# Strassen's seven products for eight in the second feed-forward's first weights, with the tokens in two passes

## The chip, the cores and the metric

The kernel runs on one core of a Trainium2 chip. The metric is the device time in microseconds (us); three runs of the kernel before give 2407.78, 2408.85 and 2410.29, median 2408.85. The engines are TensorE (PE; PEld is its weight load), VectorE (DVE), ScalarE (ACT), GpSimd (POOL) and SyncE (SP), whose queue issues the DMA transfers.

## The reference

Attention over 4 batches of 8 heads, 576 positions of 64, masked by blocks of 64; then two feed-forwards on 2304 tokens of 512 values. The change touches the last one alone: eight experts, all of them on every token, weighted by a matrix P that eight rounds of row and column normalisation make of the logits.

```
logits = x @ w_gate                         # 2304 x 8
P = exp(logits - logits.max())
for _ in range(8):
    P /= P.sum(1, keepdims=True) + 1e-09
    P /= P.sum(0, keepdims=True) + 1e-09
    P *= N / E
for e in range(8):
    h = np.maximum(x @ w1[e], 0.0)          # 512 -> 1024
    out += P[:, e:e + 1] * (h @ w2[e])      # 1024 -> 512
```

## The kernel before

**Numbers.** Products run in fp32r. Each operand is split into a high part (a copy to fp32r, `copy`, line 274 on ScalarE, 278 on VectorE) and a low part (what is left, `minus`, line 287 on GpSimd or VectorE). A product is three matmuls, high by high, high by low, low by high (`THREE`).

**Order.** Every operation is put into a graph with its engine, an estimated duration and the buffers that it reads and writes. `Graph.emit` then makes the order of each engine by a list schedule, twelve times forward and backward, and keeps the shortest by its own estimates. An operation with alternatives goes to the engine on which it would end first. So the order of every engine is fixed before the run, each works through its own in order, and waits for others by semaphores. Buffers are rings: the next use of a ring's tile waits for the users of the one before.

**The second feed-forward, `moe2`.** The 2304 tokens lie in five blocks (512, 512, 512, 384, 384), with the 512 values as four chunks of 128 partitions, in the tiles `acc`. `split_x2` makes high and low parts of all five blocks, `x2`. The weights come in 32 rounds: 8 experts by 4 groups `g`, each of two slices `f` of 128 hidden values. A round loads four tiles of 128 x 512 (two of w1, two of w2; ring `raw`, 3 tiles) by SP and splits them (`Loader.get`; ring `w`, 9 tiles). Then, for each block:

- `up` (its matmuls on line 881, in `xw`): for each `f`, 4 chunks by 3 terms = 12 matmuls into one PSUM bank `ps`, as wide as the block; then ScalarE's relu writes the high part of `h` (line 1088) and VectorE its low part (line 1090).
- `down` (line 1103), one block behind: for each 128 tokens 6 matmuls of 512 columns into a bank `pm`, which VectorE multiplies by P and adds into `acc` (line 1118). So `acc` first holds x and then the output.

The `logits` (line 1022) are made of the split x as 16 rows and turned back by transposes (line 1032). `sink` makes P during the first rounds.

Of the kernel before, what the change touches and what calls it, by code (L numbers as in the profile page):

```python
# [8 lines left out]
F32 = mybir.dt.float32  # L9
# [181 lines left out]
def t_act(n, psum=False, ap=0):  # L191
    return (50 if psum else 92) + n / 1.2 + 90 * ap


def t_v1(n):
    return 66 + n / 0.96
# [19 lines left out]
def tile_attn_moe_moe2(ctx: ExitStack, tc: tile.TileContext, qT, kT, vP, wg, wv, wo, rg, gw, w1, w2, ident_d, mq_d, mk_d, bm_d, out):  # L216
# [14 lines left out]
    def f32(ap):  # L231
        return ap.bitcast(F32)
# [736 lines left out]
    def late_buf(make, par=False):  # L969
        b = Buf(late(make), par=par)  # L970
        b.before = set(att_ops)
        return b

    def moe2():
        x2 = []
        for j in range(NB):
            n = BL[j]
            if j < NB - 1:
                b = late_buf(lambda p, j=j, n=n: p.tile([128, 2 * NK * n], F32R, name=f"x2_{j}"), par=True)
            else:  # L980
                b = XT.next(par=True)
            x2.append(b)
        gwr = late_buf(lambda p: p.tile([128, NK, E], F32, name="gwr"))
        gws = late_buf(lambda p: p.tile([128, NK, 128], F32R, name="gws"))
        onec = late_buf(lambda p: p.tile([128, 128], F32, name="onec"))
        lg = late_buf(lambda p: p.tile([128, TT, 2 * E], F32, name="lg"), par=True)
        Pm = late_buf(lambda p: p.tile([128, TT, E], F32, name="Pm"))
        sm1 = late_buf(lambda p: p.tile([128, TT], F32, name="sm1"))
        sm8 = late_buf(lambda p: p.tile([128, E], F32, name="sm8"))
        sc1 = late_buf(lambda p: p.tile([128, 8], F32, name="sc1"))  # L990
        lt_t = late(lambda p: p.tile([2 * E, 512], F32, name="lt"))
        LT = Ring([lt_t])

        def x2v(j):
            return x2[j]()[:, 0 : 2 * NK * BL[j]].rearrange("p (c k n) -> p c k n", c=2, k=NK)

        def split_x2(j):
            for k in range(NK):
                hi = Buf(x2[j].get)
                hi.before = x2[j].before  # L1000
                src = accb[j][k]
                h_ = lambda k=k: x2v(j)[:, 0, k]
                copy(G.op, BL[j], h_, src, r=[src], w=[hi])
                x2[j].writes |= hi.writes
                x2[j].users |= hi.writes
                minus(G.op, BL[j], lambda k=k: x2v(j)[:, 1, k], src, lambda h_=h_: f32(h_()), r=[src, hi], w=[x2[j]])

        G.op("SP", 100, lambda: nc.sync.dma_start(out=gwr(), in_=gw), w=[gwr], lat=2000)
        G.op("DVE", 300, lambda: nc.vector.memset(f32(gws()), 0.0), w=[gws])
        G.op("DVE", 100, lambda: nc.vector.memset(onec(), 1.0), w=[onec])  # L1010
        G.op("ACT", t_act(32), lambda: nc.scalar.activation(out=gws()[:, :, 0:E], in_=gwr(), func=AF.Copy), r=[gwr, gws], w=[gws])
        G.op("DVE", t_v1(32), lambda: nc.vector.tensor_tensor(
            out=gws()[:, :, E : 2 * E], in0=gwr(), in1=f32(gws()[:, :, 0:E]), op=ALU.subtract), r=[gwr, gws], w=[gws])

        def logits(j):
            n, nt, t0 = BL[j], BL[j] // 128, B0[j] // 128
            ps, lt = PO.next(), LT.next()

            def go():
                for k in range(NK):  # L1020
                    for c in range(2):
                        nc.tensor.matmul(out=ps()[:, 0:n], lhsT=gws()[:, k, :], rhs=x2v(j)[:, c, k, :],  # L1022
                                         start=k == 0 and c == 0, stop=k == NK - 1 and c == 1)

            G.op("PE", 8 * t_mm(n), go, r=[gws, x2[j]], w=[ps], prio=1.0)
            G.op("ACT", t_act(n, True), lambda: nc.scalar.activation(out=lt()[:, 0:n], in_=ps()[0 : 2 * E, 0:n], func=AF.Copy),
                 r=[ps], w=[lt])
            pt = PO.next()

            def tp():  # L1030
                for t in range(nt):
                    nc.tensor.transpose(out=pt()[:, 2 * E * t : 2 * E * (t + 1)], in_=lt()[:, 128 * t : 128 * t + 128],
                                        identity=ident_t[0 : 2 * E, 0 : 2 * E])

            G.op("PE", 110 * nt, tp, r=[lt, ident], w=[pt], prio=1.0)
            G.op("ACT", 150, lambda: nc.scalar.activation(
                out=lg()[:, t0 : t0 + nt, :], in_=pt()[:, 0 : 2 * E * nt].rearrange("p (t e) -> p t e", t=nt), func=AF.Copy),
                r=[pt], w=[lg])

        def sink():  # L1040

            V = nc.vector

            def first():
                V.tensor_tensor(out=Pm(), in0=lg()[:, :, 0:E], in1=lg()[:, :, E : 2 * E], op=ALU.add)
                V.tensor_reduce(out=sc1()[:, 0:1], in_=Pm().rearrange("p t e -> p (t e)"), axis=AX, op=ALU.max)

            G.op("DVE", 500, first, r=[lg], w=[Pm, sc1])
# [7 lines left out]
            G.op("ACT", 1600, lambda: nc.scalar.activation(out=Pm(), in_=Pm(), func=AF.Exp, bias=sc1()[:, 2:3], scale=1.0),  # L1056
                 r=[Pm, sc1], w=[Pm])
# [21 lines left out]

        accc = [[fixed(acc[j][:, DM * t : DM * t + DM]) for t in range(BL[j] // 128)] for j in range(NB)]  # L1080

        def up(e, g, j, ws):
            n, hs = BL[j], []
            xv = lambda: x2v(j)
            for w in ws:
                ph, ht = PS.next(), HT.next()
                xw(ph, w, [x2[j]] * NK, xv, n, 2.0)
                G.op("ACT", t_act(n, True), lambda ph=ph, ht=ht: nc.scalar.activation(  # L1088
                    out=ht()[:, 0, 0:n], in_=ph()[:, 0:n], func=AF.Relu), r=[ph], w=[ht])
                G.op("DVE", t_v1(n), lambda ph=ph, ht=ht: nc.vector.scalar_tensor_tensor(  # L1090
                    out=ht()[:, 1, 0:n], in0=ph()[:, 0:n], scalar=0.0, in1=f32(ht()[:, 0, 0:n]),
                    op0=ALU.max, op1=ALU.subtract), r=[ph, ht], w=[ht])
                hs.append(ht)
            return hs

        def down(e, g, j, hs, ws):
            for t in range(BL[j] // 128):
                tt, dst, y = B0[j] // 128 + t, accc[j][t], PM.next()

                def go(t=t, y=y):  # L1100
                    for q, ht in enumerate(hs):
                        for a, c in THREE:
                            nc.tensor.matmul(  # L1103
                                out=y(), lhsT=ht()[:, a, 128 * t : 128 * t + 128], rhs=ws[q]()[:, c, :],
                                start=q == 0 and (a, c) == (0, 0), stop=q == len(hs) - 1 and (a, c) == (1, 0))

                G.op("PE", 3 * len(hs) * t_mm(512), go, r=[*hs, *ws], w=[y], prio=2.0)
                if e == 0 and g == 0:
                    G.op("ACT", t_act(512, True), lambda y=y, dst=dst: nc.scalar.activation(out=dst(), in_=y(), func=AF.Copy),
                         r=[y], w=[dst], after=x2[j].writes)  # L1110
                elif e == 0:
                    G.op("DVE", t_v1(512), lambda y=y, dst=dst: nc.vector.tensor_tensor(out=dst(), in0=y(), in1=dst(), op=ALU.add),
                         r=[y, dst], w=[dst])
                else:
                    if e == 1 and g == 0:
                        G.op("DVE", 63 + t_v2(512), lambda dst=dst, tt=tt: nc.vector.tensor_scalar_mul(
                            out=dst(), in0=dst(), scalar1=Pm()[:, tt, 0:1]), r=[dst, Pm], w=[dst])
                    G.op("DVE", 63 + t_v1(512), lambda y=y, dst=dst, tt=tt, e=e: nc.vector.scalar_tensor_tensor(  # L1118
                        out=dst(), in0=y(), scalar=Pm()[:, tt, e : e + 1], in1=dst(), op0=ALU.mult, op1=ALU.add),
                        r=[y, dst, Pm], w=[dst])  # L1120
                if e == E - 1 and g == NG - 1:
                    G.op("SP", 1100, lambda dst=dst, tt=tt: nc.sync.dma_start(out=out[128 * tt : 128 * tt + 128, :], in_=dst()), r=[dst])

        pend = None
        for e in range(E):
            for g in range(NG):
                fs = range(GF * g, GF * g + GF)
                w1s = [L.get(w1[e, f], None, False, 0.5) for f in fs]
                w2s = None
                for j in range(NB):  # L1130
                    if e == 0 and g == 0:
                        split_x2(j)
# [67 lines left out]
```

## Time and profile before

| | |
|---|---|
| median of three runs | 2408.85 us |
| the profiled execution, its own time | 2405.6 us |
| its span, first to last instruction | 2403.8 us |
| mean granted TensorE clock | 0.982 |
| PE busy | 2340.4 us, 97% |
| VectorE, ScalarE, GpSimd busy | 1250.0, 632.2, 488.6 us |

The profile shows one execution. Its time and its span differ by what lies around the instructions. Busy shares are means over stages with different limits: in the first third of the span the attention keeps VectorE, ScalarE and GpSimd busy too, from about 800 us on the second feed-forward runs. Matmuls are pipelined, so the duration of one (some 0.4 us for 512 columns) is longer than the step from one start to the next; the price of a matmul is read from starts.

### The profile page before, as it was taken

To read this page: it belongs to the slowest core of one execution; us is meant where nothing else is said; L and a number is where in the kernel's file an instruction comes from. 1 tells how busy PE (TensorE), PEld (TensorE's weight loads), DVE (VectorE), ACT (ScalarE), POOL (GpSimd) and SP (SyncE) were. 2 spreads that over 40 slices of the span, in tenths; PEclk is the share of its full clock that TensorE was granted. 3 is DMA by queue.
4 is the path that set the end of the run, shared out by engine and by line. 5 is a ranking of instruction groups with operands and counts; after the bars stand their busy time and mean duration, and the time that the engine had idled before them with its cause. 6 is when DMAs were issued, how large, how long until landed. Compare 5 with 4: busy or idle time off the path is not lost.

```text
span 2403.8 us, 28223 instructions
## 1 busy us (share of the span) xinstructions
PE 2340.4 (97%) x10918; PEld 1963.0 (82%) x10918; DVE 1250.0 (52%) x2162; ACT 632.2 (26%) x1359; POOL 488.6 (20%) x405
## 2 busy tenths in 40 slices
PE   8789889999999999999999999999999999999999
PEld 5567667888899888888888888888888888888887
DVE  8899987876533623543333433344433443333444
ACT  3566655454212321111111111111111111111110
POOL 5565653422311211000110001100011001110000
PEclk8889999999999999999999999999999999999999
DMA  5544566453576100000000000000000000000002
GB/s 155 153 152 153 185 193 215 152 167 115 201 234 232 48 27 18 27 18 18 27 23 22 18 18 27 27 18 18 18 27 27 18 18 18 27 27 18 18 1 79
DMA packets 70970, 177.76 MB, mean 74 GB/s; under 512 B 12842, under 2 KB 16170, under 8 KB 70836
## 3 DMA queue, kind: packets, MB, share of 16 engines
q1 hardware_dynamic: 70836, 175.96, 23.3%
q8 instruction: 86, 1.41, 0.2%
q14 instruction: 48, 0.39, 0.1%
HBM read 152.33 MB, written 23.59 MB: 73 GB/s over the span
## 4 chain that ended last, share of the span: by engine, by line
PE 84%; DVE 6%; issue 1%; DMA 0%; ACT 0%; POOL 0%; SPq 0%; DVEq 0%; POOLq 0%
PE ps L881 33%; PE pm L1103 33%; PE pm L881 9%; PE pm L912 5%; PE ps L657 1%; PE ps L457 1%; DVE p L649 1%; PE po L700 1%; DVE mn L465 1%; DVE acc L334 1%; DVE ptl L664 1%; DVE acc L336 0%; DVE acc L921 0%; DVE rs L640 0%; PE po L1022 0%
## 5 line engine op out<-in xcount | busy, mean ns | idle before, releaser
L881 PE MATMUL ps<-x,w 128*128 128x512 f32 (+1 forms) x3840 | 835.1, 372 | 0.0
L1103 PE MATMUL pm<-w,h 128*128 128x512 f32 x3456 | 815.7, 391 | 0.0
L881 PEld LDWEIGHTS ps<-x,w 128*128 128x128 f32 x3840 | 703.6, 188 | 108.3
L1103 PEld LDWEIGHTS pm<-w,h 128*128 128x128 f32 x3456 | 647.6, 188 | 136.1
L1090 DVE SCALAR_TENSOR_TENSOR h<-ps,h 128x512 fp32r<-128x512 f32 (+1 forms) x320 | 204.1, 638 | 675.8 <-ACT h L1088 673.6
L1118 DVE SCALAR_TENSOR_TENSOR acc<-pm,Pm,acc 128x512 f32<-128x512 f32 x504 | 378.5, 751 | 242.8 <-PE pm L1103 239.0
L1088 ACT ACTIVATE h<-ps 128x512 fp32r<-128x512 f32 (+1 forms) x320 | 177.6, 555 | 1231.7 <-PE ps L881 1231.7
L287 POOL TENSOR_TENSOR w<-raw,w 128x512 fp32r<-128x512 f32 x161 | 211.6, 1322 | 1382.2 <-ACT w L274 1341.9
L881 PE MATMUL pm<-x,w 128*128 128x512 f32 (+1 forms) x1440 | 335.3, 378 | 2.9 <-POOL x L287 1.3
L881 PEld LDWEIGHTS pm<-x,w 128*128 128x128 f32 x1440 | 258.5, 191 | 35.6 <-DVE acc L921 1.7
L912 PE MATMUL pm<-h,w 128*128 128x512 f32 (+1 forms) x720 | 164.9, 377 | 3.8 <-DVE t L896 1.5
L912 PEld LDWEIGHTS pm<-h,w 128*128 128x128 f32 x720 | 131.6, 192 | 21.7 <-DVE t L896 2.0
L274 ACT ACTIVATE w<-raw 128x512 fp32r<-128x512 f32 x164 | 102.6, 627 | 89.9 <-PE pm L1103 83.4
L287 POOL TENSOR_TENSOR h<-t,h 128x512 fp32r<-128x512 f32 (+1 forms) x56 | 69.2, 1237 | 186.3 <-ACT h L274 178.5
L465 DVE TENSOR_REDUCE mn<-ps 128x1 f32<-128x512 f32 (+4 forms) x159 | 72.9, 474 | 19.5 <-PE ps L457 18.7
L472 ACT ACTIVATE p<-ps,mn 128x128 f32<-128x128 f32 (+3 forms) x142 | 72.5, 517 | 35.5 <-DVE mn L465 28.4
L657 PE MATMUL ps<-ident,p 128*128 128x128 f32 (+1 forms) x370 | 76.2, 291 | 3.6 <-DVE p L649 3.5
L896 DVE SCALAR_TENSOR_TENSOR t<-t,pm 128x512 f32<-128x512 f32 (+1 forms) x60 | 37.6, 627 | 79.4 <-ACT t L894 79.2
L921 DVE TENSOR_TENSOR acc<-pm,acc 128x512 f32<-128x512 f32 (+1 forms) x100 | 63.1, 632 | 28.4 <-PE pm L912 25.9
L657 PEld LDWEIGHTS ps<-ident,p 128*128 128x128 f32 (+1 forms) x370 | 48.7, 148 | 32.5 <-issue 10.2
L457 PE MATMUL ps<-ka,qa 128*128 128x512 f32 (+3 forms) x150 | 54.0, 369 | 11.2 <-DVE ptl L664 7.3
L663 ACT ACTIVATE pth<-ps 128x128 fp32r<-128x128 f32 (+2 forms) x99 | 48.9, 501 | 59.1 <-PE ps L657 54.0
(208 smaller groups left out, 1529.6 us busy)
## 6 DMA issues: line engine op xcount, KB each, us to landing
raw<-w_dram SPq DMA_DIRECT2D x128, 256.0 KB, 2.6
w<-kg SPq DMA_DIRECT2D x48, 512.0 KB, 3.9
w<-kv SPq DMA_DIRECT2D x48, 512.0 KB, 3.7
w<-ko SPq DMA_DIRECT2D x48, 512.0 KB, 3.5
rq<-qT_dram SPq DMA_DIRECT2D x56, 144.0 KB, 3.6
rq<-kT_dram SPq DMA_DIRECT2D x52, 144.0 KB, 3.7
acc<-wg_dram SPq DMA_DIRECT2D x12, 512.0 KB, 4.2
acc<-wv_dram SPq DMA_DIRECT2D x12, 512.0 KB, 4.4
```

The lines of the kernel that those rows point to most:

```text
L274: nc.scalar.activation(out=out_(), in_=in_(), func=AF.Copy, scale=scale)
L287: eng.tensor_tensor(out=out_(), in0=a(), in1=b(), op=ALU.subtract)
L457: nc.tensor.matmul(out=ps()[:, o : o + n], lhsT=a[:, 128 * t : 128 * t + 128], rhs=c[:, k0 : k0 + n], start=start, stop=stop)
L465: return A("DVE", t_v1(n), lambda: nc.vector.tensor_reduce(out=m()[:, col : col + 1], in_=ps()[:, o : o + n], axis=AX, op=ALU.max, negate= ...
L472: A("ACT", t_act(n, True, 2), lambda: nc.scalar.activation(out=p()[:, c0 : c0 + n], in_=ps()[:, o : o + n], func=AF.Exp, bias=m()[:, t : t ...
L657: A("PE", 109 if n > 64 else 58, lambda: nc.tensor.transpose(out=ps()[:, o : o + n], in_=p()[0:n, k0 : k0 + 128], identity=ident_t[0:n, 0:n]),
L881: nc.tensor.matmul(out=ps()[:, 0:n], lhsT=w()[:, a, 128 * k : 128 * k + 128], rhs=xv()[:, c, k, 0:n], start=k == 0 and (a, c) == (0, 0), s ...
L912: nc.tensor.matmul(out=ps()[:, 0:n], lhsT=wos[q]()[:, a, 128 * m : 128 * m + 128], rhs=ht()[:, c, 0:n], start=q == 0 and (a, c) == (0, 0), ...
L1088: G.op("ACT", t_act(n, True), lambda ph=ph, ht=ht: nc.scalar.activation(out=ht()[:, 0, 0:n], in_=ph()[:, 0:n], func=AF.Relu), r=[ph], w=[ht])
L1090: G.op("DVE", t_v1(n), lambda ph=ph, ht=ht: nc.vector.scalar_tensor_tensor(out=ht()[:, 1, 0:n], in0=ph()[:, 0:n], scalar=0.0, in1=f32(ht() ...
L1103: nc.tensor.matmul(out=y(), lhsT=ht()[:, a, 128 * t : 128 * t + 128], rhs=ws[q]()[:, c, :], start=q == 0 and (a, c) == (0, 0), stop=q == l ...
L1118: G.op("DVE", 63 + t_v1(512), lambda y=y, dst=dst, tt=tt, e=e: nc.vector.scalar_tensor_tensor(out=dst(), in0=y(), scalar=Pm()[:, tt, e : e ...
```

## The change

Two slices `f` of w1 (256 hidden values) by the 512 inner values are seen as 2 x 2 blocks of 128-row pairs, two token blocks as the two columns of the other matrix. Seven block products (`m(0)` to `m(6)`) with sums of blocks replace the eight:

- Tokens run in two passes over all experts: blocks 0 and 1 (512 columns each) in the first, blocks 3 and 4 (384 each) and the two halves of block 2 (256 each) in the second. Every weight tile is loaded and split in each pass.
- `operands` makes, for each pair of blocks, seven operands (three differences first, line 1032 in `add`, then high and low parts) into `xs`; the second pass uses the same tiles again, and the tile `x_84`.
- `weights1` makes four sums of blocks of w1 (tiles `sp`) and splits four tiles in place of two.
- `up` computes the products (line 1187) into three banks X, Y, Z. X gathers three products in turn; its partial sums are copied out by ScalarE (`keep`, line 1196) and added to Y and Z by VectorE (`plus`, line 1201). Relu is on line 1207, the low part on 1209.
- `down` is as before (line 1243, accumulation on line 1258), for the tokens of the pass. PSUM banks: four for `up`, three for `down`.
- The `logits` are 72 plain float32 matmuls of 8 columns (line 1105) on the unsplit x.

```
-        def up(e, g, j, ws):
-            n, hs = BL[j], []
-            for w in ws:
-                ph, ht = PS.next(), HT.next()
-                xw(ph, w, [x2[j]] * NK, xv, n, 2.0)
...
+    PASSES = [[((0, 0), (1, 0), 512)], [((3, 0), (4, 0), 384), ((2, 0), (2, 256), 256)]]
...
+                b11, b12, b21, b22 = b(0, 0), b(1, 0), b(0, 1), b(1, 1)
+                t1 = diff(b12, b11)
+                t2 = diff(b22, t1)
+                t3 = diff(b22, b12)
+                for i, x in ((0, b11), (1, b21), (2, b22), (4, t1), (5, t2), (6, t3)):
+                    split(i, *x)
+                split(3, *diff(b21, t2))
...
+            add(256, sv_[0], a21, a22, r=[r1], w=[s[0]], **k)
+            add(256, sv_[1], sv_[0], a11, op=ALU.subtract, r=[s[0], r0], w=[s[1]], **k)
+            add(256, sv_[2], a11, a21, op=ALU.subtract, r=[r0, r1], w=[s[2]], **k)
+            add(256, sv_[3], a12, sv_[1], op=ALU.subtract, r=[r0, s[1]], w=[s[3]], **k)
+            ws = []
+            for src, b, n in ((r0, [r0], 512), (lambda: r1()[:, 256:512], [r1], 256), (p0, s[0:2], 512), (p1, s[2:4], 512)):
...
+            return [(wa, 0), (wa, 256), (wd, 256), (wb, 0), (wc, 0), (wc, 256), (wd, 0)]
...
+            X, Y, Z = UP.next(), UP.next(), UP.next()
...
+                    for k in range(2):
+                        for a, c in THREE:
+                            nc.tensor.matmul(
+                                out=bank()[:, 0:n], lhsT=w()[:, a, o + 128 * k : o + 128 * k + 128], rhs=views[p, q, i, k, c](),
+                                start=start and k == 0 and (a, c) == (0, 0), stop=k == 1 and (a, c) == (1, 0),
+                                skip_group_check=not start)
...
+            m(0, X)
+            s1 = keep(X)
+            m(1, Y)
+            h11 = relu(plus(Y, s1))
+            m(5, X)
+            s2 = keep(X)
+            m(4, Z)
+            m(6, X)
+            s3 = keep(X)
+            h22 = relu(plus(Z, s3))
+            m(3, X)
+            h21 = relu(X, True)
+            m(2, Z)
+            h12 = relu(plus(Z, s2))
```

PE in the order before, in a round of the second feed-forward: blocks 0 and 1 of x (`x_0`, `x_1`), the banks `ps` and `pm`, the weights `w_70`, `w_71` (w1) and `w_68`, `w_69` (w2).

```order
L881 MATMUL ps_95<-x_0_5117,w_70 128x512 x12
L881 MATMUL ps_93<-x_0_5117,w_71 128x512 x12
L1103 MATMUL pm_89<-w_68,h_80 128x512 x3
L1103 MATMUL pm_89<-w_69,h_81 128x512 x3
L1103 MATMUL pm_90<-w_68,h_80 128x512 x3
L1103 MATMUL pm_90<-w_69,h_81 128x512 x3
L1103 MATMUL pm_91<-w_68,h_80 128x512 x3
L1103 MATMUL pm_91<-w_69,h_81 128x512 x3
L881 MATMUL ps_94<-x_1_5109,w_70 128x512 x12
L881 MATMUL ps_95<-x_1_5109,w_71 128x512 x12
```

PE in the order of the changed kernel, in a round of the first pass: the `xs` are the operands of the products 0, 1, 5, 4, 6, 3, 2 in this order, `ps_94` is X, `ps_95` Y, `pm_92` Z.

```order
L1187 MATMUL ps_94<-xs_5118,w_67 128x512 x6
L1187 MATMUL ps_95<-xs_5109,w_67 128x512 x6
L1187 MATMUL ps_94<-xs_5154,w_69 128x512 x6
L1187 MATMUL pm_92<-xs_5141,w_69 128x512 x6
L1187 MATMUL ps_94<-xs_5129,w_70 128x512 x6
L1243 MATMUL pm_90<-w_74,h_78 128x512 x3
L1243 MATMUL pm_90<-w_66,h_80 128x512 x3
L1187 MATMUL ps_94<-xs_6287,w_68 128x512 x6
L1187 MATMUL pm_92<-xs_5148,w_70 128x512 x6
L1243 MATMUL pm_91<-w_74,h_78 128x512 x3
L1243 MATMUL pm_91<-w_66,h_80 128x512 x3
```

Groups of 12 into one bank have become groups of 6 into three, X is written four times with one product or one token tile of the round before between; the other token tiles follow the block. The next round's third product reads `w_66`, which the last token tile ahead of that round has just used.

ScalarE before, in a round: the relus of `ps` into `h`, and two weight conversions.

```order
L1088 ACTIVATE h_78<-ps_93 128x512
L1088 ACTIVATE h_79<-ps_94 128x512
L274 ACTIVATE w_69<-raw_77 128x512
L274 ACTIVATE w_70<-raw_75 128x512
L1088 ACTIVATE h_80<-ps_95 128x512
L1088 ACTIVATE h_81<-ps_93 128x512
```

ScalarE in a round of the first pass: `ct` are the copies of X (`pm_92` here), `sp` the sums of w1, `x_85` four more tiles of `h`.

```order
L274 ACTIVATE w_72<-sp_6245 128x512
L274 ACTIVATE w_71<-raw_75 128x256
L1196 ACTIVATE ct_5116<-pm_92 128x512
L1207 ACTIVATE x_85<-ct_5116 128x512
L1196 ACTIVATE ct_5132<-pm_92 128x512
L274 ACTIVATE w_67<-raw_75 128x512
L1196 ACTIVATE ct_5156<-pm_92 128x512
L274 ACTIVATE w_70<-sp_5135 128x512
L1207 ACTIVATE x_85<-ct_5156 128x512
L1207 ACTIVATE x_85<-pm_92 128x512
L274 ACTIVATE w_71<-raw_77 128x512
L1207 ACTIVATE x_85<-ct_5132 128x512
```

The three copies of X have come in, and stand behind weight conversions: the first behind two, the third behind `w_67`, which waits for its load.

## Rows read from the trace of the kernel before

**Rows 1.** The page: busy time, share, instructions by engine; granted TensorE clock by slice.
```profile
PE 2340.4 (97%) x10918; PEld 1963.0 (82%) x10918; DVE 1250.0 (52%) x2162; ACT 632.2 (26%) x1359; POOL 488.6 (20%) x405
...
PEclk8889999999999999999999999999999999999999
```

**Rows 2.** The page: the chain that ended last, share of the span by line.
```profile
PE 84%; DVE 6%; issue 1%; DMA 0%; ACT 0%; POOL 0%; SPq 0%; DVEq 0%; POOLq 0%
PE ps L881 33%; PE pm L1103 33%; PE pm L881 9%; PE pm L912 5%; PE ps L657 1%; PE ps L457 1%; DVE p L649 1%; PE po L700 1%; DVE mn L465 1%; DVE acc L334 1%; DVE ptl L664 1%; DVE acc L336 0%; DVE acc L921 0%; DVE rs L640 0%; PE po L1022 0%
```

**Rows 3.** Timeline of PE, a round: start us, us, engine, line, operation.
```profile
1108.35 5.78 PE L881 MATMUL ps<-x,w 128*128 128x512 f32 x24
1113.96 5.64 PE L1103 MATMUL pm<-w,h 128*128 128x512 f32 x24
1119.44 5.76 PE L881 MATMUL ps<-x,w 128*128 128x512 f32 x24
...
1130.51 4.40 PE L881 MATMUL ps<-x,w 128*128 128x384 f32 x24
1134.75 5.64 PE L1103 MATMUL pm<-w,h 128*128 128x512 f32 x24
...
1148.54 1.80 PE L881 MATMUL ps<-x,w 128*128 128x512 f32 x7
...
1198.43 4.83 PE L881 MATMUL ps<-x,w 128*128 128x512 f32 x20
```

**Rows 4.** Timeline of PE and its weight loads, 256-wide matmuls of the attention.
```profile
440.77 0.19 PEld L457 LDWEIGHTS ps<-ka,qa 128*128 128x128 f32 x1
440.80 0.36 PE L457 MATMUL ps<-ka,qa 128*128 128x256 f32 x1
440.88 0.19 PEld L457 LDWEIGHTS ps<-kb,qb 96*128 96x128 f32 x1
441.00 0.28 PE L457 MATMUL ps<-kb,qb 96*128 96x256 f32 x1
...
441.12 0.40 PE L881 MATMUL pm<-x,w 128*128 128x512 f32 x1
...
527.46 0.29 PE L457 MATMUL ps<-kb,qb 96*128 96x256 f32 x1
...
527.59 0.58 PE L657 MATMUL ps<-ident,p 128*128 128x128 f32 x3
```

**Rows 5.** Lines 1022, 763: min/median/max of one, first to last start; timeline.
```profile
L1022 PE MATMUL po<-x,gws x40: 331/389/399, 681.1 to 805.3; 128*128 128x512 f32 x24, 128*128 128x384 f32 x16
...
455.34 1.17 PE L763 MATMUL ps<-ones,ss 128*128 128x1 f32 x10
456.37 0.48 PE L881 MATMUL pm<-x,w 128*128 128x512 f32 x1
...
L763 PE MATMUL pm<-ones,ss x10: 352/352/372, 124.1 to 126.0; 128*128 128x1 f32 x10
```

**Rows 6.** ScalarE's timeline; groups of ScalarE, VectorE and GpSimd (busy us, mean ns).
```profile
1111.36 0.60 ACT L1088 ACTIVATE h<-ps 128x512 fp32r<-128x512 f32 x1 [2.13 <-PE ps L881]
...
L274 ACT ACTIVATE w<-raw 128x512 fp32r<-128x512 f32 x164 | 102.6, 627 | 89.9 <-PE pm L1103 83.4 <-PE pm L881 2.7 <-DMA raw<-w_dram 1.3
...
L1118 DVE SCALAR_TENSOR_TENSOR acc<-pm,Pm,acc 128x512 f32<-128x512 f32 x504 | 378.5, 751 | 242.8 <-PE pm L1103 239.0
...
L287 POOL TENSOR_TENSOR w<-raw,w 128x512 fp32r<-128x512 f32 x161 | 211.6, 1322 | 1382.2 <-ACT w L274 1341.9
```

**Rows 7.** The loads into `raw` in the second feed-forward, issue to landing.
```profile
DMA to landing us min/median/max: 2.4/2.6/4.3
```

**Rows 8.** Timeline: a VectorE subtraction of two SBUF inputs alone, another beside GpSimd.
```profile
243.82 0.68 DVE L287 TENSOR_TENSOR w<-raw,w 128x512 fp32r<-128x512 f32 x1
...
319.13 1.47 POOL L287 TENSOR_TENSOR w<-raw,w 128x512 fp32r<-128x512 f32 x1
...
319.38 1.78 DVE L287 TENSOR_TENSOR h<-t,h 128x512 fp32r<-128x512 f32 x1
```

More of the change, by code (lines that the diff above doesn't have):

```diff
@@ L972, in late_buf, with ring_of, next_ @@
         return b
-    def moe2():
[L975 to L982, printed above, removed]
+    def ring_of(tiles_, before):
+        r = Ring(tiles_)
+        plain = r.next
+        def next_(par=False):
+            k = len(r)
+            b = plain(par)
+            if k < r.n:
+                b.before |= before[k]
+            return b
+        r.next = next_
+        return r
@@ L990, in moe2, with raw_x @@
         sc1 = late_buf(lambda p: p.tile([128, 8], F32, name="sc1"))
[L991 to L1006, printed above, removed]
+        def raw_x(j, c, m, n):
+            return acc[j][:, m * BL[j] + c : m * BL[j] + c + n]
@@ L1015, in logits @@
         def logits(j):
             n, nt, t0 = BL[j], BL[j] // 128, B0[j] // 128
-            ps, lt = PO.next(), LT.next()
+            ps = PO.next()
             def go():
[L1020 to L1030, printed above, removed]
                 for t in range(nt):
-                    nc.tensor.transpose(out=pt()[:, 2 * E * t : 2 * E * (t + 1)], in_=lt()[:, 128 * t : 128 * t + 128],
-                                        identity=ident_t[0 : 2 * E, 0 : 2 * E])
-            G.op("PE", 110 * nt, tp, r=[lt, ident], w=[pt], prio=1.0)
+                    for k in range(NK):
+                        nc.tensor.matmul(out=ps()[:, E * t : E * t + E], lhsT=raw_x(j, 128 * t, k, 128), rhs=gwr()[:, k, :],
+                                         start=k == 0, stop=k == NK - 1)
@@ L1102, in go, with up, m @@
+        def up(p, q, xs, ws):
+            n = PASSES[p][q][2]
+            X, Y, Z = UP.next(), UP.next(), UP.next()
+            first = set()
+            def m(i, bank):
+                w, o = ws[i]
+                start = bank not in first
+                first.add(bank)
+                def go():
+                    for k in range(2):
                         for a, c in THREE:
                             nc.tensor.matmul(
-                                out=y(), lhsT=ht()[:, a, 128 * t : 128 * t + 128], rhs=ws[q]()[:, c, :],
@@ L1105, in go @@
[L1105 to L1120, printed above, removed]
```

197 lines of the change are left out of this document (150 added, 47 removed).

## Prediction

> **What bounds the kernel now.** I read the totals and the clock slices first: TensorE (PE) is busy 97% of the span and its clock stays at the 2.4 GHz level through the whole second feed-forward [rows 1]. Then the chain of waits: 84% of it is PE, and its two heaviest entries are the second feed-forward's two kinds of product, line 881 (rows of w1 against x) and line 1103 (h against w2) [rows 2]. Then the timeline of PE in one round, a pair of 128-wide slices of one expert: the rows follow each other with no idle time, and from the same place of one round to the next it is 1198.43 - 1148.54 = 49.89 us [rows 3]. So in this stage every nanosecond that PE streams is on the path, and the other engines matter only where PE waits for them, which it does not now.
>
> **What the products cost.** From start to start [rows 3]: 24 matmuls of 512 columns on line 881 take 1113.96 - 1108.35 = 5.61 us, 24 of 384 take 4.24 us, 24 on line 1103 take 5.48 us. A round of before has 72 + 48 of line 881 and 108 of line 1103: 3 x 5.61 + 2 x 4.24 + 4.5 x 5.48 = 49.97 us, as measured (49.89).
>
> **What the change removes.** With Strassen's seven products a round has 42 matmuls for each pair of token blocks (7 products, 2 halves of the inner length, 3 high/low terms) where four quarters by eight products took 48. First pass, 512 columns: 42/24 x 5.61 = 9.82 us, and its 8 token tiles of line 1243, as line 1103 now, 2 x 5.48 = 10.96: 20.78 us. Second pass, pairs of 384 and of 256 columns: 42/24 x 4.24 = 7.42, 42 matmuls of 256, and 10 tiles = 2.5 x 5.48 = 13.70.
>
> The 256-wide matmul does not occur in this stage. In the attention one runs from 441.00 to the next start at 441.12, another from 527.46 to 527.59: 0.12 and 0.13 us. A third row has 0.20 us (440.80 to 441.00), but there the weight load (440.88) starts late behind two narrow matmuls, one load following another after 0.11 us [rows 4]; in a steady stream a load of 0.11 us fits under a 256-wide stream. I take 0.125, with 0.12 and 0.20 as the ends: 42 x 0.125 = 5.25 us. Second pass 26.37, both 47.15 us against 49.97; 2.82 us saved in each of 32 rounds is 90 us (97 at 0.12, 84 at 0.13, a loss of 11 at 0.20).
>
> The Trainium skill ("TensorE: Matmul & The Clock Gate", Part 3, The mechanism) says that a weight load overlaps running matmuls only where the row groups differ, which would put load and stream of full-height matmuls behind each other; the 512-wide rows of this trace (0.23 us each with a load between) speak against it. By that rule the third rival below would hold.
>
> **Logits.** The 40 matmuls on line 1022 become 72 in plain float32, 8 columns wide. Their price: line 763 has the same weights with one column, and its 10 records (two to an instruction) take 456.37 - 455.34 = 1.03 us, 0.103 each. 144 x 0.103 = 14.8 us on PE, less 24 x 0.228 + 16 x 0.177 = 8.3: +6 us. Whether the clock holds through such narrow stretches no row shows; at the lower level, where PE had waited before, 10 records took from 124.1 to 126.0, 0.19 to 0.21 each [rows 5], so +15 us is the upper end. I add 1.
>
> **The new waits inside a block of products.** Three partial sums in one PSUM bank X must be copied by ScalarE (line 1196) before the next product adds to it. Now ScalarE starts 0.20 us after a product's stream ends (1108.35 + 5.61/2 = 1111.16; it starts at 1111.36) and takes 0.60 [rows 3, 6]; the cover is one other product, 6 x 0.234 = 1.40 us at 512, 1.06 at 384, and two of 0.75 at 256. Worst is the first copy of the first pass: ahead of it on ScalarE stand two weight conversions (0.63 and, by width, some 0.4) and a relu (0.63) that may start only as the block does: 0.20 + 1.66 + 0.60 = 2.46 us against 2.80 of cover. The other two places have a token tile of line 1243 (1.37 us) put between by the order. VectorE does in a half round 8 accumulations at 0.75 and 8 operations at 0.68 or less, about 11 of 20.8 us; GpSimd 5 subtractions at 1.32 and 4 of half width, about 9 us [rows 6, 8]. None is near a bound.
>
> **Weights.** All are loaded and split twice, and w1 gets four sums of blocks. The tight loop is in the first pass: the tile for the third product is the w2 tile that the last token tile of the half round before has just used. Copy 0.63 + subtraction 1.32 after 0.20 is 2.15 us; it is wanted after two products and two matmuls of the third, 3.3 us. From there on: one half-width subtraction, then a load lands in 2.6 us (at most 4.3) [rows 7], so at about 2.9 + 2.7 = 5.6 us, its conversion ends at 6.3, and the copy of X behind it on ScalarE is wanted at 7.2. Queued behind that copy are the relus of the same block and the next weights. A slow load (4.3) costs 0.8 us there once. SP's queue, which issues the loads in order, holds only weights there, each waiting for its own buffer. I take 6 us for all waits of 64 half rounds (0 to 70, the far end of rival 1).
>
> **Ends of the passes.** The operands of the second pass go into the buffers of the first, one by one as the last block frees them. GpSimd has some 20 operations in the 28 us until the last one is wanted (by width from 1.32: 17 us), so a few us of margin: 2 us, up to 20. At the start 28 splits and 8 differences take the place of the 40 splits of x2 beside the first feed-forward: 3 us, 0 to 15.
>
> **The sum** against the profiled execution, 2405.6 us (span 2403.8): -90 + 6 + 1 + 6 + 2 + 3 = -72, 2333.6. The median of the runs shown is 2408.85, 3.25 above it: **2337 us**.
>
> **Rivals.**
> 1. VectorE and GpSimd hold each other up. A subtraction with both inputs in SBUF takes 0.68 us alone (243.82) and 1.78 beside a GpSimd operation (319.38 against 319.13) [rows 8]. Now line 1090 reads one input from PSUM; afterwards three of four such operations, and the sums of weights, read both from SBUF while GpSimd is busy some 45% of the time. Each delay is up to 1.1 us, the margins above are 0.3 to 1.2; if each half round loses 0.7 us in place of 0.1, that is +39: 2376 (at 0.3, 2350; at 1.1, 2401). Against it: those operations stand outside the chain of X, apart from the one ahead of the sum for the last product, which has about 1.2 us. The Trainium skill ("SBUF — State Buffer", Who interferes with whom) states it as a rule: VectorE's second SBUF input comes through the port it shares with GpSimd and whoever starts first blocks the other. The trace agrees, 1.78 against 0.68.
> 2. The two changes of pass cost 30 us instead of 5, because copies, differences and normal conversions pile up on one engine: 2362.
> 3. Slower: in the long stream of 256-wide matmuls the weight load does not hide and each costs the 0.20 us of the third row. 1344 x 0.075 = +101: 2437. It decides from 0.125 + 72/1344 = 0.179 us on. For it: the row itself, and that the load's 0.11 leaves only 0.01 of cover. Against it: 0.12 and 0.13 where the stream was steady.
> 4. It does not do what it says: conversions twice over make PE wait over 1.1 us in every half round (64 x 1.1 = 72), and seven products give what eight gave: 2409. Against it, the engines' loads above.
>
> **Chances.** The forecast 0.65 (own range 2322 to 2352); rival 1 0.17, rival 2 0.10, rival 3 0.05, rival 4 0.03. To leave out no more than 2 in 10 the range takes in most of rivals 1 and 2: 2319 to 2382. 0.2%, about 5 us, is what a measurement of this kernel can tell from no change. Faster 0.91 (the forecast, rivals 1 and 2), same 0.03 (rival 4), slower 0.06 (rival 3, and the far end of the others).
>
> **What would show it.** A first-pass half round of PE of 20.8 us and a second-pass one of 26.4; 256-wide matmuls of line 1187 at 0.12 to 0.13 us from start to start (0.20: rival 3); PE's idle time before line 1187 put down to ScalarE, VectorE or GpSimd adding to under 15 us (40 or more, with VectorE's line 1209 well over 0.68 us: rival 1); a gap of PE between the last 512-wide and the first 384-wide product (over 15 us: rival 2); line 1105 at 14.8 us and the granted clock at 2.4 GHz behind it. The prediction is wrong if the round saves other than 2.6 to 3.0 us, or if the waits hold more than the saving.

## The result, and the profile after

The changed kernel takes **2328.34 us** (median of four runs, 2328.03 to 2329.95) against 2409.57 for the kernel before on the same chip (four runs, 2407.78 to 2410.9): a ratio of 0.9665, 95% interval 0.9648 to 0.9681. The forecast was 2337, range 2319 to 2382. The profiled execution took 2328.22 us, its span is 2326.4 (before 2403.8).

The page of the changed kernel, totals, clock slices and the chain by line, as [rows 1, 2] show them of before:

```profile
PE 2254.6 (97%) x11196; PEld 1924.3 (83%) x11196; DVE 1511.3 (65%) x2558; ACT 916.1 (39%) x1990; POOL 986.7 (42%) x909
...
PEclk8788999999999999999999999999999999999999
...
PE 85%; DVE 12%; issue 2%; ACT 0%; DMA 0%; POOL 0%; SPq 0%; DVEq 0%; ACTq 0%; POOLq 0%
```

PE is still busy 97%, with less to do. VectorE's part of the chain has doubled, from 6 to 12% [rows 2], but of these 281 us 250 lie ahead of 860 us, most of them in the attention, where PE's own time hardly changes ("all else" in the table below); the other 30 lie at the change of pass, between 1440 and 1490 us, and none in the steady rounds. First these rounds, PE's timeline in the changed kernel (start, duration, line, tiles, count). A half round of the first pass:

```profile
1016.75 1.52 PE L1187 MATMUL ps<-xs,w 128*128 128x512 f32 x6
1018.11 1.56 PE L1187 MATMUL pm<-xs,w 128*128 128x512 f32 x6
1019.50 4.26 PE L1187 MATMUL ps<-xs,w 128*128 128x512 f32 x18
1023.60 1.52 PE L1243 MATMUL pm<-w,x 128*128 128x512 f32 x6
1024.96 2.94 PE L1187 MATMUL ps<-xs,w 128*128 128x512 f32 x12
1027.74 9.70 PE L1243 MATMUL pm<-w,x 128*128 128x512 f32 x42
1037.28 1.07 PE L1187 MATMUL ps<-xs,w 128*128 128x512 f32 x4
```

From 1016.75 to 1037.28 it is 20.53 us, 42 matmuls on line 1187 and 8 token tiles, with no idle time. A round of the second pass, cut:

```profile
2003.69 5.41 PE L1187 MATMUL ps<-xs,w 128*128 128x384 f32 x30
...
2016.54 0.52 PE L1187 MATMUL pm<-xs,w 128*128 128x256 f32 x3
2016.89 0.52 PE L1187 MATMUL pm<-x,w 128*128 128x256 f32 x3
2017.25 0.52 PE L1187 MATMUL ps<-xs,w 128*128 128x256 f32 x3
...
2029.79 1.23 PE L1187 MATMUL ps<-xs,w 128*128 128x384 f32 x6
```

It takes 26.10 us, and three 256-wide matmuls 0.35 to 0.36 us, 0.12 each. So a round of both passes is 46.63 us, against 49.89 [rows 3]: 3.26 saved, 104 us in 32 rounds. But the span fell by only 77.4. To find the rest I added up, for each line of PE, the steps from one matmul's start to the next, waits included (us; e1, e2 and e10 are experiments below):

| | before | after | e1 | e2 | e10 |
|---|---|---|---|---|---|
| products with w1 (line 881 of the second feed-forward, 1187) | 809.2 | 714.9 | 803.0 | 710.1 | 706.4 |
| products with w2 (1103, 1243) | 788.9 | 790.9 | 786.2 | 791.4 | 790.3 |
| logits and their transposes (1022, 1032; 1105) | 9.9 | 16.5 | 16.5 | 15.9 | 15.1 |
| first feed-forward (881, 912) | 489.8 | 496.4 | 492.4 | 494.1 | 491.7 |
| all else, attention above all | 299.5 | 301.2 | 302.9 | 302.5 | 303.2 |
| sum | 2397.4 | 2319.9 | 2400.9 | 2314.0 | 2306.7 |

The second feed-forward's products saved 92 of the 104 us. About 8 went at the change of pass and about 5 in the first round (steps above those of the steady rounds; the kernel before has 1.6 of such steps itself). Outside, logits took 6.5 and the first feed-forward 6.6 more.

**The change of pass.** PE's timeline in the changed kernel there; in brackets the idle time ahead of a row and what ended it:

```profile
1456.28 1.56 PE L1187 MATMUL ps<-xs,w 128*128 128x512 f32 x6
1460.28 2.93 PE L1187 MATMUL pm<-xs,w 128*128 128x512 f32 x6 [2.44 <-DVE ct L1201]
...
1477.96 2.01 PE L1187 MATMUL ps<-xs,w 128*128 128x384 f32 x10 [0.86 <-POOL w L287]
1481.71 1.31 PE L1187 MATMUL ps<-xs,w 128*128 128x384 f32 x6 [1.74 <-ACT ct L1196]
```

These 5.0 us are all the idle time that the page shows before line 1187, and behind the first of them six 512-wide matmuls take 2.72 us in place of 1.36: the granted clock is 0.50, the 1.2 GHz level, from 1461 to 1463, after PE had stood idle. Windows there (stretch, length, PE busy and its instructions, granted clock, DMA share, GB/s):

```profile
1461.00:1462.00 1.00, 1.00 (x4) 0.50 0.37 141
1462.00:1463.00 1.00, 1.00 (x3) 0.50 0.00 0
```

VectorE ahead of that; the last row is the one that PE waited for:

```profile
1456.26 1.50 DVE L287 TENSOR_TENSOR w<-raw,w 128x512 fp32r<-128x512 f32 x1
1457.68 1.08 DVE L287 TENSOR_TENSOR xs<-ct,xs 128x384 fp32r<-128x384 f32 x1
1458.68 0.94 DVE L287 TENSOR_TENSOR xs<-acc,xs 128x256 fp32r<-128x256 f32 x1
1459.54 0.68 DVE L1201 TENSOR_TENSOR ct<-pm,ct 128x512 f32<-128x512 f32 x1
```

The sum on line 1201 frees PE's bank, but stands behind low parts of the second pass's operands that take 0.94 to 1.08 us where the same widths take 0.41 and 0.55 when GpSimd is idle as they start, and behind a weights' low part of 1.50. An estimate from these rows: with 0.41, 0.55 and the 0.68 of [rows 8] the sum would have started 1.9 us sooner, most of the 2.44. Line 287 on VectorE from 1430 to 1500 us, the two largest of five groups that make 20 low parts of the second pass's operands (ns min/median/max, first to last start):

```profile
L287 DVE TENSOR_TENSOR xs<-acc,xs x7: 940/1096/1409, 1450.4 to 1474.1; 128x384 fp32r<-128x384 f32 x5, 128x256 fp32r<-128x256 f32 x2
L287 DVE TENSOR_TENSOR xs<-ct,xs x7: 594/1076/1401, 1457.7 to 1475.6; 128x384 fp32r<-128x384 f32 x6, 128x256 fp32r<-128x256 f32 x1
```

**The clock at the logits.** Windows of the changed kernel, as above:

```profile
776.00:784.00 8.00, 8.00 (x52) 0.81 0.46 166
784.00:792.00 8.00, 8.00 (x38) 0.76 0.22 69
...
808.00:816.00 8.00, 8.00 (x50) 0.79 0.11 33
816.00:824.00 8.00, 8.00 (x36) 0.79 0.21 66
```

PE is busy all the time and still drops to the lower level, each time at the end of, behind or between stretches of 24 or 32 records on line 1105 (two records to a matmul). Before, the clock was 1.00 from 656 us on.

### The profile page after: what moved, and what is told of

Same layout as the page of the kernel before. It is cut to its first block, busy times and chain, and to the rows that moved or that the text cites. A ratio compares the mean times of both kernels' runs of the same rounds, so it can differ in the third digit from the quotient of the medians.

```text
span 2326.4 us, 30454 instructions
## 1 busy us (share of the span) xinstructions
PE 2254.6 (97%) x11196; PEld 1924.3 (83%) x11196; DVE 1511.3 (65%) x2558; ACT 916.1 (39%) x1990; POOL 986.7 (42%) x909
## 4 chain that ended last, share of the span: by engine, by line
PE 85%; DVE 12%; issue 2%; ACT 0%; DMA 0%; POOL 0%; SPq 0%; DVEq 0%; ACTq 0%; POOLq 0%
PE pm L1243 33%; PE ps L1187 23%; PE pm L881 10%; PE pm L1187 7%; PE pm L912 5%; PE ps L457 2%; PE ps L657 2%; DVE mn L465 1%; DVE p L649 1%; PE po L700 1%; DVE xs L287 1%; DVE acc L334 1%; DVE acc L336 1%; PE po L1105 1%; DVE ptl L664 0%
## 5 line engine op out<-in xcount | busy, mean ns | idle before, releaser
L1187 PE MATMUL ps<-xs,w 128*128 128x384 f32 (+2 forms) x2640 | 547.7, 351 | 2.6 <-ACT ct L1196 1.7
L1187 PEld LDWEIGHTS ps<-xs,w 128*128 128x128 f32 x2640 | 468.0, 189 | 55.0 <-ACT ct L1196 2.4
L1243 PE MATMUL pm<-w,h 128*128 128x512 f32 x1920 | 460.1, 391 | 0.0
L287 POOL TENSOR_TENSOR w<-raw,w 128x512 fp32r<-128x512 f32 (+1 forms) x288 | 354.2, 1236 | 178.8 <-ACT w L274 175.5
L1243 PEld LDWEIGHTS pm<-w,h 128*128 128x128 f32 x1920 | 354.6, 188 | 69.9 <-DVE acc L1258 0.4
L287 POOL TENSOR_TENSOR w<-sp,w 128x512 fp32r<-128x512 f32 x128 | 173.0, 1352 | 542.4 <-ACT w L274 542.4
L1243 PE MATMUL pm<-w,x 128*128 128x512 f32 x1536 | 366.8, 391 | 0.0
L1243 PEld LDWEIGHTS pm<-w,x 128*128 128x128 f32 x1536 | 287.3, 188 | 56.9
L274 ACT ACTIVATE w<-raw 128x512 fp32r<-128x512 f32 (+1 forms) x292 | 164.8, 576 | 26.6 <-DMA raw<-w_dram 19.9
L1187 PE MATMUL pm<-xs,w 128*128 128x512 f32 (+2 forms) x720 | 157.1, 343 | 2.4 <-DVE ct L1201 2.4
```

Of the source, the lines that this page charges most:

```text
L274: nc.scalar.activation(out=out_(), in_=in_(), func=AF.Copy, scale=scale)
L287: eng.tensor_tensor(out=out_(), in0=a(), in1=b(), op=ALU.subtract)
L1187: nc.tensor.matmul(out=bank()[:, 0:n], lhsT=w()[:, a, o + 128 * k : o + 128 * k + 128], rhs=views[p, q, i, k, c](), start=start and k == 0 ...
L1243: nc.tensor.matmul(out=y(), lhsT=hs[f][half]()[:, a, 128 * t : 128 * t + 128], rhs=ws[f]()[:, c, :], start=f == 0 and (a, c) == (0, 0), st ...
```

## The experiments

**e1: two passes, eight products.** What the two passes, with the new logits, do without Strassen. `ws` are the two slices of w1; the loop on `top, bot` runs over the two token blocks, each with the two halves of its inner length.

```
-                t1 = diff(b12, b11)
...
-                for i, x in ((0, b11), (1, b21), (2, b22), (4, t1), (5, t2), (6, t3)):
+                for i, x in ((0, b11), (1, b21), (2, b22), (3, b12)):
                     split(i, *x)
-                split(3, *diff(b21, t2))
...
-            m(0, X)
...
-            h12 = relu(plus(Z, s2))
...
+            for w in ws:
+                row = []
+                for top, bot in ((0, 1), (3, 2)):
+                    X = UP.next()
+                    m(w, 0, top, X, True)
+                    m(w, 256, bot, X, False)
+                    row.append(relu(X, True))
```

> The two passes alone, with eight plain block products in place of seven: no sums of blocks, four operands instead of seven, 48 matmuls per pair instead of 42. Theory (the saving is the seventh of the w1 products that falls away, and nothing else in the change gains anything): half round of the first pass 48 x 0.228 + 10.96 = 21.9 us, round of the second 48 x (0.1765 + 0.1195) + 13.7 = 27.9 us, together 49.8 against 46.63; 32 x 3.2 = 102 us more than the changed kernel, less 0 to 8 us that the sums cost at the start and at the change of pass: 2422 to 2431 us, slower than the kernel before. Rival (the two passes themselves bring part of the saving, since line 1187's 512-wide products run at 0.228 us against 0.234 of line 881): 2409 or less.

Measured: 2407.93, ratio to before 0.9992 (0.9982 to 1.0002): without Strassen the rest of the change gains and loses nothing in sum, and the rival (2409 or less) came out. PE's timeline in e1, a half round of the first pass and a round of the second:

```profile
1001.22 8.42 PE L1167 MATMUL ps<-xs,w 128*128 128x512 f32 x36
...
1023.07 8.42 PE L1167 MATMUL ps<-xs,w 128*128 128x512 f32 x36
...
2009.36 6.44 PE L1167 MATMUL ps<-xs,w 128*128 128x384 f32 x36
...
2037.12 6.44 PE L1167 MATMUL ps<-xs,w 128*128 128x384 f32 x36
```

21.85 + 27.76 = 49.61 us a round, near the 49.8 expected. Strassen saves 49.61 - 46.63 = 2.98 of it, 95 us in 32 rounds, and 79.6 by the medians. My theory had the saving of a round right and was wrong twice: the passes bring 9 us of products by themselves (809.2 + 788.9 against 803.0 + 786.2), which about pay for the logits and the rest, and Strassen's own price outside the steady rounds is 15 us, where I had said 0 to 8.

**e2: logits in pieces.** Same matmuls, 18 pieces of 8 records, each bracketed by two neighbouring products.

```
-            def go():
-                for t in range(nt):
+            for t in range(nt):
+                def go(t=t):
...
-            read_x[j].add(G.op("PE", 220 * NK * nt, go, r=[gwr, *accb[j]], w=[ps], prio=1.0))
+                a, b = gaps.pop(0)
+                o = G.op("PE", 220 * NK, go, r=[gwr, *accb[j]], w=[ps], prio=1.0, after={a})
+                b.deps.add(o)
+                read_x[j].add(o)
```

> The same logits, but the five stretches of 24 or 32 narrow matmul records on line 1105 are cut into 18 pieces of 8 records, each put between two wide products. Theory (the granted clock falls to 1.2 GHz behind long narrow stretches: three times, at 781, 812 and 818 us, some 12 us at half speed, 6 us lost): the clock stays at 1.00 from 660 to 830 us and the time falls by 5 to 7 us, to 2321 to 2323. Rival (the clock falls there for another reason, such as the end of the first feed-forward): falls of the same length, 2328 within 2.

Measured: 2322.43 (2322.27 to 2323.54), ratio 0.9644 (0.963 to 0.9659). The same windows in e2:

```profile
776.00:784.00 8.00, 8.00 (x48) 1.00 0.85 314
784.00:792.00 8.00, 8.00 (x51) 1.00 0.56 203
...
808.00:816.00 8.00, 7.10 (x38) 1.00 0.13 33
816.00:824.00 8.00, 8.00 (x44) 1.00 0.20 68
```

The three falls are gone and 5.9 us with them, 4.8 of it in the products with w1 (about 3 in their first round, where two of the falls had been). The theory holds as far as this goes: cut into pieces the same matmuls leave the clock up, and the wide products no longer pay. The rival fails, since the first feed-forward ends in e2 too. That every long stretch lowers the clock is not shown (last section).

**e3: some operands early.** The 256-wide pair's second half of the inner length is made ahead of expert 2.

```
-                got.append(operands(pair, place))
+                got.append(operands(pair, place, (0,) if q else (0, 1)))
...
+                if (p, e) == (0, 2):
+                    operands_early()
```

> Of the 72 operations that make the second pass's operands, the 18 of the 256-wide pair's second half of the inner length (they have a buffer of their own) are put in front of expert 2 of the first pass. Theory (the 5.0 us of idle PE and 1.7 us of low clock at the change of pass come from VectorE's and GpSimd's pile of splits, 1.1 to 1.5 us each on VectorE beside GpSimd): half of the loss goes, 2324 to 2326. Rival (the loss comes from buffers being freed one by one, whatever else the engines have to do): the waits stay, 2328 within 2.

Measured: 2328.74, ratio 0.9671 (0.9656 to 0.9685), no difference. At the change of pass idle time is 4.6 us for 5.0, the excess of the steps 6.1 for 8.1; what that gives goes in longer logits (18.0 us). By itself inconclusive.

**e4: GpSimd idle.** The weights' sums and low parts on VectorE in experts 1 to 6 of each pass.

```
+        if far:
+            k.pop("margin")
+            return op("DVE", t_v1(n), lambda: go(nc.vector), **k)
...
+            far = 1 <= e <= 6
```

> In experts 1 to 6 of both passes the sums and low parts of the weights are made on VectorE, so that GpSimd is idle there. Theory (VectorE and GpSimd do hold each other up, but outside the chain that PE waits for): line 1209 with SBUF inputs falls from 0.8 to 0.68 us at 512 columns, VectorE is busy about 18.5 of the 20.5 us of a half round, and the time stays, 2328 within 4. Rival 1 (the hold-ups cost something in every half round): faster by 5 us or more. Rival 2 (VectorE, fuller, is late for PSUM banks): slower by over 10 us.

Measured: 2329.83, ratio 0.9674 (0.9659 to 0.9688): the same time. VectorE's groups between 900 and 1400 us (count, busy us, mean ns), in the changed kernel:

```profile
L1209 DVE SCALAR_TENSOR_TENSOR h<-ct,h 128x512 fp32r<-128x512 f32 x28 | 34.0, 1215 | 6.3 <-ACT h L1207 6.3
...
L1209 DVE SCALAR_TENSOR_TENSOR h<-ps,h 128x512 fp32r<-128x512 f32 x13 | 8.9, 688 | 0.7 <-ACT h L1207 0.3
```

and in e4:

```profile
L1216 DVE SCALAR_TENSOR_TENSOR h<-ct,h 128x512 fp32r<-128x512 f32 x28 | 19.9, 710 | 7.0 <-ACT h L1214 7.0
...
L1216 DVE SCALAR_TENSOR_TENSOR h<-ps,h 128x512 fp32r<-128x512 f32 x13 | 9.0, 691 | 2.2 <-ACT h L1214 2.2
```

With both inputs in SBUF the operation takes 1.2 us where GpSimd is busy 186 of 400 us (1000 to 1400) and 0.71 where it is busy 15; with one input in PSUM 0.69 in both. That is what the Trainium skill ("SBUF — State Buffer", Who interferes with whom) says of the second SBUF input; the trace agrees. So rival 1's mechanism is there in full, and in the steady rounds it costs nothing: a half round of the first pass takes 20.53 us in e4 too (1019.79 to 1040.32). My 18.5 us of VectorE in a half round were too many: 287.6 busy us of 400, 14.8 in 20.53, since the hold-ups had been in the 253.8 of the changed kernel.

**e5: 256-wide matmuls in halves.** The sums of that pair come out different in it; every matmul is there.

```
+                            for z, m_ in ((0, 128), (128, 128)) if n == 256 else ((0, n),):
+                                nc.tensor.matmul(
+                                    out=bank()[:, z : z + m_], lhsT=w()[:, a, o + 128 * k : o + 128 * k + 128],
+                                    rhs=views[p, q, i, k, c]()[:, z : z + m_],
```

> Each 256-wide matmul of line 1187 is cut into two of 128 columns with the same weights, each with a weight load of its own: 84 in place of 42 in a round of the second pass. Theory (a weight load runs beside the stream before it, and its 0.11 us from load to load is the floor of the step): 0.11 us each, 84 x 0.11 = 9.2 us in place of 5.0, +4.2 us a round, +135 us: about 2463. Rival (a load waits for the end of the stream): 0.11 + 0.055 = 0.165 us each, 13.9 us, +283: about 2611. Rival (loads cost nothing at this width): 0.06 each, no change, 2328.

Measured: 2469.36 in one run, 141 us more than the changed kernel. PE in e5:

```profile
2015.00 0.83 PE L1188 MATMUL ps<-xs,w 128*128 128x128 f32 x6
2015.67 0.83 PE L1188 MATMUL ps<-x,w 128*128 128x128 f32 x6
```

0.67 us for six, 0.11 each: the step from load to load of [rows 4]. That is the theory's figure: the load runs beside the stream ahead of it and sets the step at 128 columns, while 256 columns take 0.12, above the load's 0.11. So the third rival had no ground at 256 columns. By the Trainium skill's rule ("TensorE: Matmul & The Clock Gate", Part 3, The mechanism: overlap only between different row groups) load and stream would add up, an estimate of 0.165 each (0.11 for the load and 0.055 for the stream, about half a 256-wide step); the run's 0.11 speaks against it.

**e6 and e7: tiles 32 bytes lower.** The 512-wide step of line 881 was 233.4 ns in the second feed-forward of before, of line 1187 229 after, and of line 881 in the first feed-forward 227 where the other engines were idle. Same instructions, same order, other addresses:

```
         G.emit()
+        c_pool[0].tile([128, 8], F32, name="pad")
```

> The kernel before, same instructions in the same order, with 32 bytes of unused memory behind the tiles of the second feed-forward, so that four of the five x2 tiles start 32 bytes lower: their start addresses, multiples of 64 before, become 32 above one, as those of the w tiles and of the fifth x2 tile are. Theory (where the streamed tile starts decides between the two steps of a matmul: in the kernel before the 384-wide ones of the fifth tile take 174.4 ns from start to start, those of the fourth 176.7, and the 512-wide ones 233.4): line 881 falls to about 227 ns at 512 and 174.4 at 384 columns in the second feed-forward, 2304 x 0.0065 + 768 x 0.0023 = 17 us, 2392. Rival (the longer step comes from the bank, from other engines or from chance): the same step and 2409.

Measured: 2401.23, ratio 0.9967 (0.9955 to 0.998). PE in e6, blocks 1 to 3:

```profile
1111.82 5.67 PE L881 MATMUL ps<-x,w 128*128 128x512 f32 x24
1117.33 5.65 PE L1103 MATMUL pm<-w,h 128*128 128x512 f32 x24
1122.82 5.76 PE L881 MATMUL ps<-x,w 128*128 128x512 f32 x24
1128.42 5.62 PE L1103 MATMUL pm<-w,h 128*128 128x512 f32 x24
1133.88 4.32 PE L881 MATMUL ps<-x,w 128*128 128x384 f32 x24
1138.04 5.61 PE L1103 MATMUL pm<-w,h 128*128 128x512 f32 x24
```

Block 1 takes 5.51 us where it took 5.61 [rows 3], block 3 4.16 for 4.24; block 2 has 5.60 as before, and so has block 0. So where a tile starts does count, but not by the rule that I gave, which would have moved all four: of the gain of 17 us 8.6 came by the medians and 6.0 by the steps of line 881 (809.2 to 803.2).

> The changed kernel, same instructions in the same order, with 32 bytes of unused memory behind the late tiles, so that the seven xs tiles start at a multiple of 64 bytes and not 32 above one. Theory (as for the kernel before with its tiles moved, the other way round): 512-wide steps of line 1187 go from 229 to 233 to 234 ns, 384-wide from 174.6 to 176.7, half of the 256-wide by 1 to 3 ns: 1344 x 0.005 + 1344 x 0.002 + 672 x 0.002 = 11 us, 2336 to 2341. Rival: no difference, 2328.

Measured: 2328.3, ratio 0.9663 (0.965 to 0.9676), no difference: the 512-wide steps of line 1187 did go to 233.4 ns, but the 384-wide ones stayed, the 256-wide ones fell by 1.0 and those of line 1243 in the second pass by 1.3. Which addresses make the longer step stays open.

**e8: e2 and e3 together.**

> The changed kernel with both edits: logits in 18 pieces, and the 256-wide pair's second half of operands made in front of expert 2. Theory (the two losses are in different places, 6 us behind the logits and some 8 at the change of pass, of which early operands took 2 in the profile of that run): 2320. Rival (what is won at one place is lost at the other through the order that the scheduler makes): 2322 or more.

Measured: 2321.75 (2319.3 to 2324.48), ratio 0.9636 (0.9623 to 0.965): not to be told from e2.

**e9: no operands for the second pass.**

```
-            xs = pass_operands(p)
...
+                                views[1, q, i, k, c] = lambda v=views[0, 0, i, k, c], n=pair[2]: v()[:, 0:n]
+                xs = [xs[0]] * len(pairs)
```

> The changed kernel without the 72 operations that make the second pass's operands: its products read the first pass's operands (so the second pass computes with the wrong tokens; every matmul is there). Theory (the loss at the change of pass, 5.0 us of idle PE and about 3 at the low clock, is the price of these operations on VectorE and GpSimd): PE goes on without a gap from the last 512-wide product to the 384-wide ones, 32 x 46.63 us for the rounds, 8 us less: 2320. Rival (it is the change itself, to other widths, banks and tokens, that makes PE wait): 2326 or more.

Measured: 2323.99 (2321.84 to 2325.85), ratio 0.9648 (0.9635 to 0.9661). PE in e9 at the change:

```profile
1460.14 1.55 PE L1187 MATMUL pm<-xs,w 128*128 128x512 f32 x6
1461.53 9.70 PE L1243 MATMUL pm<-w,h 128*128 128x512 f32 x42
1471.07 2.29 PE L1187 MATMUL ps<-xs,w 128*128 128x384 f32 x12
```

No idle time and no low clock are left there: the loss is the price of these operations, not of the change to other widths and banks. The products with w1 take 8.3 us less; the time falls by 4.4 (5.8 between the two profiles), in part since this run's logits take 18.0 us and the clock falls more often there.

**e10 and e11: the plan learns of the hold-ups.** Both on e8.

```
-        return op("POOL", t_pool(n), lambda: go(nc.gpsimd), alts=[("DVE", t_v1(n), lambda: go(nc.vector))], **k)
+        return op("POOL", t_pool(n), lambda: go(nc.gpsimd), alts=[("DVE", t_v1(n) + slow, lambda: go(nc.vector))], **k)
...
-                    read_x[ja].add(minus(G.op, n, lv, a, lambda: f32(hv()), r=[src, hb], w=[lb]))
+                    read_x[ja].add(minus(G.op, n, lv, a, lambda: f32(hv()), r=[src, hb], w=[lb], slow=700.0 if n < 512 else 0.0))
```

The last line is e10's; e11 leaves `t_v1(n)` as it was and has in its place:

```
+                    read_x[ja].add(minus(G.op, n, lv, a, lambda: f32(hv()), r=[src, hb], w=[lb], margin=GAIN if n < 512 else 0.0))
```

> As e8_both (2321.75), and the scheduler is told that a low part of the second pass's operands takes 0.7 us more on VectorE, about what the trace shows of it beside GpSimd (1.1 to 1.5 us where it reckons with 0.47 at 384 columns); 11 of them go to GpSimd. Theory (the plan fails at the change of pass because it does not know of the hold-ups): half of the remaining 6 us of waits there go, 2318 to 2320. Rival (GpSimd is late in its turn, or the order of other things shifts): 2321 or more.

> As e8_both, and VectorE is given a low part of the second pass's operands only where GpSimd would end it over 1.5 us later; the durations in the plan are as before. Theory (fewer operations on VectorE are enough): 2318 to 2320. Rival (without the true durations the plan still has VectorE late for PE's sums): as e8_both, 2321 to 2322.

Measured: e10 **2313.58** (2311.02 to 2314.97), ratio 0.9602 (0.9589 to 0.9615); e11 2315.55, 0.9609 (0.9596 to 0.9622), not to be told apart. Both are below what theory (2318 to 2320) and rival (2321 or more) gave. PE in e10, the waits that are left at the change:

```profile
1451.21 1.64 PE L1210 MATMUL pm<-xs,w 128*128 128x512 f32 x6 [0.84 <-DVE ct L1224]
...
1466.05 0.62 PE L1210 MATMUL ps<-xs,w 128*128 128x384 f32 x2 [0.20 <-ACT t L1219]
1467.49 3.05 PE L1210 MATMUL ps<-xs,w 128*128 128x384 f32 x16 [0.81 <-POOL w L287]
```

and the same groups of line 287 on VectorE in e10, from 1430 to 1500 us:

```profile
L287 DVE TENSOR_TENSOR xs<-acc,xs x4: 576/1014/1132, 1444.3 to 1460.5; 128x384 fp32r<-128x384 f32 x3, 128x256 fp32r<-128x256 f32 x1
L287 DVE TENSOR_TENSOR xs<-ct,xs x4: 490/1036/1490, 1449.2 to 1468.1; 128x384 fp32r<-128x384 f32 x2, 128x256 fp32r<-128x256 f32 x2
```

Of the low parts of the second pass's operands VectorE makes 20 in the changed kernel in this stretch, 16 in e8, 9 in e10 and 10 in e11, and PE's idle time at the change is 5.0, 4.6, 1.9 and 2.3 us. So the pile on VectorE is most of what PE waits for, and e11's theory holds against its rival: fewer operations there are enough, also with the old durations in the plan. How much of the wait is their number and how much their hold-ups was not tried apart.

At the change the steps' excess is 3.1 us in e10, for 6.1 in e8: the half that was expected. The other 5 us of e8's 8 were not: 2.4 lie in the first feed-forward (494.1 to 491.7; 1.0 of it in 20 matmuls on line 912 behind a wait of PE at 655 us, where the lower clock ends sooner: 5.30 us for 6.31), 0.8 in the logits, and the rest is between one profile and the medians. The plan is made anew as a whole, and nothing here tells which part of it gave them. e10 is 14.8 us faster than the changed kernel.

## Why the prediction was right, and where it was not

- **The products: right in kind, too small.** -90 was forecast, the steady rounds give -104, and a round saves 3.26, outside the 2.6 to 3.0 that I had set as the mark of a wrong prediction. The terms that were mis-sized: the first pass's 42 matmuls of 512 columns take 20.53 - 10.96 = 9.57 us, not 9.82, since I gave them line 881's 0.234, a step that depends on where the tile lies (e6, e7); and the 256-wide ones take 42 x 0.1195 = 5.02, not 5.25 (I took 0.125 where the lower end, 0.12, was right).
- **Logits: +6 forecast, +6.5 measured**, in part by luck: 1.6 us of transposes that I had not taken off, and some 1.3 us of low clock in line 1105 that I had not put there. At the full clock line 1105 takes 15.1 us (e10) against 14.8 from line 763 [rows 5].
- **The clock: +1 was the wrong value.** I had written that no row shows whether it holds, had an upper end of 15, and took the lower one. It fell three times; e2 prices that at 6.
- **Waits inside a block of products: +6 forecast, none found.** All 5.0 us of idle time before line 1187 are at the change of pass. The cover of one other product for ScalarE's copy, and the weights' margins, held in every steady half round.
- **The change of pass: +2 forecast, 8 measured.** The step that failed: "GpSimd has some 20 operations in the 28 us". I counted GpSimd alone. The scheduler had put most of the low parts on VectorE, 20 of 28 within 32 us, at an estimate of 0.33 and 0.47 us by width where the medians are 0.89 and 1.10, ahead of the sums that free PE's banks; e9, without them, has no wait there, and e10 and e11, with half as many on VectorE, less than half. Rival 2's place, with rival 1's mechanism, at a quarter of rival 2's price.
- **The start: +3 forecast.** The first feed-forward takes 6.6 us more and the first round of the second about 5. e2 takes 2.3 and about 3 of these away, and 1.0 is low clock behind a wait of PE ahead of the logits (20 matmuls on line 912 from 655.91 us on take 6.28 us, 5.31 before). So some half is the clock; the rest changes with the plan (492 to 496 us in the table) and was not tried by itself.
- **The sum** came out near (-77.5 by the steps, forecast -72) because errors of both signs met: 14 more from the products and 6 less for waits, against 6 more at the change of pass, 8 more for start and clock, 2 more for logits and attention; -76, and 1.5 that these rounded terms leave open. The rivals: 1 is there and hidden, 2 is a quarter of its size, 3 is refuted by e5 and by 0.12 us a matmul, 4 by the steady half rounds without a wait and by e1, where eight products take 79.6 us more. By the medians the kernel gained 81.2 us, for 71.9 forecast: the 3.25 us that I added between a profiled execution and the median were not there in the changed kernel (2328.22 and 2328.34).

## What to carry to other kernels

Where one engine is the bound, a product that is not computed is worth its full step in the steady rounds; look for what it gives back at the ends of the loops, where one-off work is pushed into queues that free that engine's buffers. A plan with estimated durations failed here where it piled work on an engine that another one holds up: give it the durations that the trace shows beside the other engine, or keep work off that engine by a margin; here either did as well. Put narrow matmuls between wide ones in small pieces rather than in a row.

## What the runs showed that was not expected

- PE busy without a gap still lost the clock: 32 records of 8 columns at 777.94 were followed by nearly seven us at 1.2 GHz, while the same 32 at 761.88 and 799.25 were not. In e9, with the same five stretches at nearly the same times, the granted clock was 0.50 behind each of them (at 766, 783, 804 and from 815 to 823 us). What makes the difference was not tried.
- The step of a 512-wide matmul differs with where the streamed tile lies, 227 and 233 to 234 ns with all other engines idle; in the first feed-forward it is 230 beside busy engines. 32 bytes moved one tile from 234.0 to 229.6 and a 384-wide one from 176.7 to 173.4, and left two others where they were.
